# Block 1 of the second token group by seven products, and another order of VectorE's steps in that group

## The chip, the cores and the metric

One of the cores of a Trainium2 chip runs the whole program. The metric is the device time in microseconds (us) of one execution; lower is better.

## The reference

Two blocks follow each other. The first is a chunked state-space layer over 4 batches, 8 heads, 768 positions, head size 32 and state size 16; the second is a feed-forward layer with the quick GELU over all 3072 tokens.

```python
# per chunk: y = (C B^T * L) x + (C state) * exp(cum);  state = decay * state + sum_j B_j x_j decay_j
x = attn_out.transpose(0, 2, 1, 3).reshape(3072, 256)
h = x @ w_in                                  # 256 -> 2048
g = h * (1.0 / (1.0 + np.exp(-1.702 * h)))
out = g @ w_out                               # 2048 -> 256
```

## The kernel before

The 3072 tokens are worked on in six groups of 512 (g = 0 to 5). Each group's rows of the state-space layer are made on TensorE (gain, score and the y steps) while the feed-forward layer of the group before is still running, so that TensorE always has full 128x128 matmuls beside the small 32-row ones. A "pair" is 256 tokens; a group has two pairs.

The feed-forward layer's first product (yT times w_in) has 16 blocks of 128 rows of the hidden layer, taken two by two as j = 0 to 7. It is computed in one of two ways.

- Directly: `hidden` (L887) makes one row block with two matmuls of 512 columns, and ScalarE applies the silu from PSUM to SBUF.
- By seven products instead of eight, on 256 columns each (Strassen's scheme in Winograd's form): `first(g, j, i)` (L931) issues one step named by its letter. Steps 1, 6, 7 and 4 accumulate in bank X, and after 1, 6 and 7 ScalarE copies the running sum out of X (into `ac` or `b`) before the next product may add to it; 4 ends with a silu from X. Steps 5, 2 and 3 accumulate in bank Y. D adds Y and `ac` on VectorE, 3 is followed by an addition of Y and `b` on VectorE, S and T are silus on ScalarE. The sums of weights that the products need come from `mix_in(n)` (L905; n covers blocks 2n and 2n + 1), and the sums of yT from `mix_y(g)` (L924).

The second product (with w_out) is done by seven products as well: `product` (L1028), shown as P in the step lists, with sums from `mix_w(n)` and `mix_g(g, j)`, accumulated in seven half banks called `acc`.

A fp32 matmul is executed as two passes; the profile counts passes.

The state-space steps of a group, by their names in the code: `decay` (a scan on VectorE and two products with b, L424 and L489), `gain` (TensorE, into two banks A), `keep_both` (ScalarE copies out of the A banks, then VectorE additions), `score` (TensorE, into the area cb), `weigh` (VectorE multiplies the decay matrix L by cb, L693), `finish(pairs, (0,))` (TensorE, states into the area y, L822), `finish(pairs, (1,))` (TensorE, weighted rows into y, L836, and then three copies of y into yT on ScalarE, L871 and L869). The areas cb, y and acc are one and the same four banks of PSUM, one after the other. `clip_rows` and `decay_rows` prepare the decay of later rows on VectorE and GpSimd, and `turn_out` (L1111) transposes a half group of results on VectorE and issues four output DMAs on SyncE's queue.

Every engine works in the order of the program: `in_order` (L21) pins each instruction behind the one before it on its engine. The order between steps is written out by hand, in strings of step names that `run` (L1290) goes through. Two places are of importance here. The dictionary `after` (L1263) holds the steps behind the direct blocks of group 1 (H0 behind block 0, H1 behind block 1). The strings of `run(1, ...)` from L1332 on hold the rest of the second group (g = 1); `steady(j)` (L1307) gives the steps for blocks 5 to 7, mixed with the second product's P.

Of the kernel before, what the change touches and what calls it, by code (L numbers as in the profile page):

```python
# [16 lines left out]
P = 128  # L17
# [18 lines left out]
def kernel(  # L36
# [383 lines left out]
    def decay(p):  # L420

        L = ssd.tile([P, 2 * NH * H], FP32, tag="L", name=f"L{p}", bufs=3)
        Ls[p] = L.rearrange("p (k r q i) -> p k r q i", k=2, r=R, q=Q)
        nc.vector.tensor_tensor_scan(  # L424
            out=L, data0=ra[p].rearrange("p k e -> p (k e)"),
            data1=idents.rearrange("p h i -> p (h i)"), initial=0.0, op0=ALU.mult, op1=ALU.add)
        for k in range(2):
            ends(p, k)
# [203 lines left out]
    def turn_blocks(g):  # L632

        t = {}
        for name in "CB":
            t[name] = ssd.tile([P, TG], FP32, tag=f"{name}t", name=f"{name}t{g}", bufs=1)
            nc.vector.transpose(
                out=t[name].rearrange("p (n i f) -> p n f i", n=PG, i=32),
                in_=blocks.pop((name, g)).rearrange("p h (f n) -> p f h n", n=N))
        for n in range(PG):  # L640
            s = st[g * PG + n] = {}
            s["BT"], s["tp"] = (
                t[name][:, n * 2 * P:(n + 1) * 2 * P].rearrange("p (k i) -> p k i", k=2)
                for name in "BC")
# [16 lines left out]
    def since_start(p, engine=nc.vector):  # L661

        b, c = divmod(2 * p, NC)
        s = st[p]
        tp = s["tp"]
        s["CsT"] = ssd.tile([P, 2, P], FP32, tag="CsT", name=f"CsT{p}", bufs=3)
        engine.tensor_tensor(out=s["CsT"], in0=tp, in1=since[b][:, c:c + 2], op=ALU.mult)

    def score(pairs, between=lambda: None, to=None):

        cb = (to or area(f"cb{pairs[0]}")).rearrange("p r (k e) -> p r k e", k=2 * PG)
        for n, p in enumerate(pairs):
            s = st[p]
            BT, CT = s["BT"], s.pop("CT")
            s["cb"] = cb[:, :, 2 * n:2 * n + 2]
            if n:
                between()
            for k in range(2):
                for i, side in enumerate(SIDES):
                    for r in range(R):  # L680
                        rows = slice(32 * r, 32 * r + 32)
                        nc.tensor.matmul(  # L682
                            out=s["cb"][side, r, k].rearrange("p (q i) -> p q i", q=Q),
                            lhsT=BT[rows, k, side], rhs=CT[rows, k, :, side],
                            start=True, stop=True, tile_position=(32 * r, H * i),
                            skip_group_check=True)

    def weigh(p, ks=(slice(0, 2),)):

        Lv = Ls[p].rearrange("p k r q i -> p k r (q i)")  # L690
        cb = st[p]["cb"].rearrange("p r k e -> p k r e")
        for k in ks:
            nc.vector.tensor_tensor(out=Lv[:, k], in0=Lv[:, k], in1=cb[:, k], op=ALU.mult)  # L693
# [7 lines left out]
    def gain(pairs, to=None):  # L701

        A = [(bank(f"A{pairs[0]}_{i}") if to is None else to[:, i, TG // 2:])[
            :, :2 * len(pairs) * Q * D].rearrange("p (k e) -> p k e", e=Q * D) for i in range(2)]
        for n, p in enumerate(pairs):
            Be = BE.pop(p)[0]
            for k in range(2):
                for r in range(R):
                    heads = slice(Q * r, Q * r + Q)
                    for i, side in enumerate(SIDES):  # L710
                        if last_chunk(p, 2 * k + i):
                            continue
                        nc.tensor.matmul(  # L713
                            out=A[i][32 * r:32 * r + 32, 2 * n + k],
                            lhsT=Be[side, k, r],
                            rhs=rx[p][side, k, heads].rearrange("p h d -> p (h d)"),
                            start=True, stop=True, tile_position=(H * i, 32 * r),
                            skip_group_check=True)
            increment[p] = [t[:, 2 * n:2 * n + 2] for t in A] if pairs[0] else A
# [27 lines left out]
    def keep_both(pairs, by_scalar=False):  # L747

        for p in pairs:
            part_of(p, range(4), by_scalar)  # L750
        for p in pairs:
            add_up(p, range(4))
# [148 lines left out]


    mixed_in, mixed_y, chain = {}, {}, {}

    def mix_in(n):  # L905

        t = wide.tile([P, PN], FP32, tag=("m", "p2")[n % 2], name=f"mi{n}").rearrange(
            "p (j s e) -> p j s e", j=2, s=4)
        w = w_in[:, 4 * n:4 * (n + 1)].rearrange("p (j i) k e -> p j i k e", i=2)
        a11, a12, a21, a22 = w[:, :, 0, 0], w[:, :, 0, 1], w[:, :, 1, 0], w[:, :, 1, 1]  # L910
        s1, s2, s3, s4 = (t[:, :, i] for i in range(4))
        for o, u, v, op in ((s1, a21, a22, ALU.add), (s2, s1, a11, ALU.subtract),
                            (s3, a11, a21, ALU.subtract), (s4, a12, s2, ALU.subtract)):
            nc.vector.tensor_tensor(out=o, in0=u, in1=v, op=op)
        for k in range(2):
            mixed_in[2 * n + k] = t[:, k]

    def mix(t, B):

# [4 lines left out]
    def mix_y(g):  # L924
        mixed_y[g] = ffn.tile([P, 4, HT], FP32, tag="my", name=f"my{g}", bufs=1)
        mix(mixed_y[g], yT[g].rearrange("p k (t e) -> p k t e", t=2))
# [184 lines left out]
    def turn_out(g, i):  # L1111

        t = out_tile(g, i).rearrange("p k e -> p (k e)")
        nc.vector.transpose(out=t, in_=sums[g][:, i].rearrange("p t e -> p (t e)"))
        rows = out[g * TG:(g + 1) * TG].rearrange("(b j) d -> j b d", j=32)
        for r in range(R):
            cols = slice(i * P + 32 * r, i * P + 32 * r + 32)
            src = t[32 * r:32 * r + 32].rearrange("p (b e) -> p b e", e=32)
            n = 2 if (g, i) == (NG - 2, 1) and r else 1
            for k in range(n):  # L1120
                bs = slice(16 // n * k, 16 // n * (k + 1))
                nc.sync.dma_start(out=rows[:, bs, cols], in_=src[:, bs])
# [106 lines left out]
    def at(places, i, *work):  # L1229
        places.setdefault(i, []).extend(work)  # L1230
# [9 lines left out]
    for i, k, c in ((2, 1, 1), (3, 2, 3), (4, 4, 7), (5, 8, 10), (6, 10, 14), (7, 14, 15)):  # L1240
# [13 lines left out]
    at(in_project[0], 10, lambda: score(pairs), lambda: gain(pairs), lambda: keep_both(pairs, True),  # L1254
       lambda: weigh(PG), lambda: weigh(PG + 1))
    at(in_project[0], 15, lambda: finish(pairs))
    at(in_project[0], 13, lambda: mix_in(1), lambda: turn_blocks(2), lambda: decay(n))
    at(in_project[0], 6, lambda: spread(n), lambda: spread(n + 1), lambda: load_blocks(n),
       lambda: load_blocks(n + 1), lambda: load(n, "b"), lambda: load(n + 1, "b"),
       lambda: load(n, "x"), lambda: load(n + 1, "x"))  # L1260
# [2 lines left out]
    after = {}  # L1263

    later = n, n + 1
    at(after, "H0", lambda: decay(n + 1), lambda: mix_y(1), lambda: since_start(n),
       lambda: since_start(n + 1), lambda: gain(later), lambda: keep_both(later, True), lambda: score(later),
       lambda: weigh(n), lambda: weigh(n + 1))
    at(after, "H1", lambda: turn_out(0, 0), lambda: turn_out(0, 1), lambda: mix_in(2),
       lambda: mix_w(0))  # L1270
    assert [b for b in range(NB) if 3 * CG <= b * NC < 4 * CG] == [2]


# [7 lines left out]
    load_blocks(p)  # L1281
    spread_rows(2)
    load(p, "bx")
    for step in "H0", "H1":
        for i in range(2):
            hidden(1, 2 * int(step[1:]) + i)
        for do in after[step]:
            do()

    def run(g, steps, products=(), **do):  # L1290


        products = iter(products)
        for step in steps.split():
            if step == "P":
                product(*next(products))
            elif step in do:
                do[step]()
            else:
                j, i = step.split(".")  # L1300
                first(g, int(j), i)
        assert next(products, None) is None
# [24 lines left out]
    def more_loads():  # L1327
# [1 line left out]
        load(p + 1)  # L1329
        spread(p + 1)  # L1330

    run(1, "2.1 3.1 2.5 2.6 3.6 z 2.2 2.7 3.5 3.7 3.2 2.D 2.4 3.D 3.4 2.S W 3.S y m 2.3 3.3 4.1 2.T 3.T",  # L1332
        m=lambda: mix_g(1, 0),
        z=lambda: finish(later, (0,)), y=lambda: finish(later, (1,)), W=lambda: clip_rows(2))
    mix_g(1, 1)
    more_loads()
    mix_in(3)
    decay_rows(2)
    run(1, "4.5 4.2 P P 4.6 P P 4.7 P P P 4.D", seven(1, 0))
    mix_w(1)  # L1340
    mix_g(1, 2)
    decay(p)
    between = {5: (lambda: mix_g(1, 3), lambda: mix_w(2)),
               6: (lambda: mix_g(1, 4), lambda: decay(p + 1)),
               7: (lambda: mix_g(1, 5), lambda: mix_w(3))}
    for j in range(5, NF // 2):
        run(1, steady(j), seven(1, j - 4), M=lambda: [do() for do in between[j]])
    k = NF // 2 - 1
    run(1, closing(k), seven(1, 4))
    mix_g(1, 6)  # L1350
    mix_in(0)
    run(1, "P P A P P P P P", seven(1, 5), A=lambda: ahead(2, p))
    mix_g(1, 7)

# [105 lines left out]
```

## Time and profile before

| what | value |
|---|---|
| median of three runs | 345.67 us (345.42 to 346.44) |
| the profiled execution, its own time | 345.17 us |
| its span, first to last instruction | 343.4 us |
| TensorE busy | 338.3 us, 98% |
| VectorE busy | 255.5 us, 74% |
| ScalarE busy | 155.8 us, 45% |
| granted TensorE clock, mean | 1.00 |

The span and the execution's own time differ by 1.8 us of start and end. The profile's times are counted from the start of the span. In this execution the first group's projection ends at about 78 us, the second group fills the stretch from there to about 124 us, and groups 2 to 5 follow.

### The profile page before, as it was taken

How to read it: one execution, taken by the hardware profiler on the slowest of the kernel's cores; microseconds unless marked ns; L12 is line 12 of the kernel's file. 1: busy time of each engine (PE TensorE's matmuls, PEld its weight loads, DVE VectorE, ACT ScalarE, POOL GpSimd, SP SyncE). 2: the span in 40 equal slices, each digit the busy share in tenths (PEclk: the TensorE clock that was granted, in tenths of full speed). 3: DMA queues.
4: the chain of work that ended last, by engine and by line, in shares of the span. 5: the costliest groups of instructions: out<-in, count | busy, mean ns of one | idle time of the engine just before them, and what ended most of it. 6: DMA issues, size and time to landing. Idle time of an engine off the chain costs nothing.

```text
span 343.4 us, 8128 instructions
## 1 busy us (share of the span) xinstructions
PE 338.3 (98%) x3378; PEld 271.2 (79%) x3378; DVE 255.5 (74%) x486; ACT 155.8 (45%) x356; POOL 13.3 (4%) x40
## 2 busy tenths in 40 slices
PE   8999999999999999999999999999999999999996
PEld 6645744555788888888888888888888888899996
DVE  6989999999999797858995667787564653465463
ACT  5798672406563314554333554342553422554320
POOL 6100010200010000000000000000000000000000
DMA  6699978455737000345513036400000300000402
GB/s 166 138 296 210 323 158 151 107 84 106 116 80 123 7 2 22 56 111 92 108 32 46 2 86 115 63 3 0 2 3 2 61 2 0 0 2 0 63 0 62
DMA packets 90020, 25.75 MB, mean 75 GB/s; under 512 B 73440, under 2 KB 87264, under 8 KB 89984
## 3 DMA queue, kind: packets, MB, share of 16 engines
q1 hardware_dynamic: 89152, 24.72, 34.8%
q8 instruction: 26, 0.43, 0.6%
q10 hardware_dynamic: 832, 0.52, 0.5%
q14 instruction: 10, 0.08, 0.1%
HBM read 21.99 MB, written 3.24 MB: 73 GB/s over the span
## 4 chain that ended last, share of the span: by engine, by line
PE 97%; DMA 1%; ACT 0%; DVE 0%; issue 0%; ACTq 0%; DVEq 0%
PE acc L1057 28%; PE X L952 19%; PE Y L962 15%; PE h L896 10%; PE o L994 8%; PE acc L1064 7%; PE y L836 3%; PE cb L682 2%; PE y L822 1%; PE A L713 1%; PE ab L556 1%; DMA az<-in_a_dram 1%; PE tp L599 0%; DVE cum L359 0%; ACT yT L856 0%
## 5 line engine op out<-in xcount | busy, mean ns | idle before, releaser
L957 ACT ACTIVATE ac<-X 128x256 f32<-128x256 f32 x76 | 29.0, 382 | 83.9 <-PE X L952 83.8
L1057 PE MATMUL acc<-mg,mw 128*128 128x256 f32 x192 | 53.9, 379 | 0.0
L1084 DVE TENSOR_TENSOR gT<-Y,ac 128x512 f32<-128x512 f32 x38 | 26.2, 689 | 37.0 <-PE Y L962 34.5
L929 ACT ACTIVATE gT<-gT 128x512 f32<-128x512 f32 (+1 forms) x76 | 38.9, 519 | 26.1 <-DVE gT L1084 25.5
L952 PE MATMUL X<-my,mi 128*128 128x256 f32 x152 | 45.1, 379 | 0.0
L1057 PEld LDWEIGHTS acc<-mg,mw 128*128 128x128 f32 x192 | 36.5, 190 | 4.9
L1084 DVE TENSOR_TENSOR gT<-Y,b 128x256 f32<-128x256 f32 x38 | 16.0, 420 | 28.7 <-PE Y L962 28.7
L896 PE MATMUL h<-yT,w_in 128*128 128x512 f32 (+1 forms) x96 | 35.1, 524 | 0.5 <-ACT yT L856 0.5
L1057 PE MATMUL acc<-gT,w_out 128*128 128x256 f32 x128 | 35.5, 379 | 0.0
L952 PEld LDWEIGHTS X<-my,mi 128*128 128x128 f32 x152 | 28.2, 190 | 3.6
L896 PEld LDWEIGHTS h<-yT,w_in 128*128 128x128 f32 x96 | 18.1, 190 | 16.0 <-issue 12.4
L994 PE MATMUL o<-gT,w_out 128*128 128x512 f32 x64 | 28.3, 596 | 0.0
L920 DVE TENSOR_TENSOR mg<-gT 128x512 f32<-128x512 f32 x40 | 27.3, 681 | 0.0
L1057 PEld LDWEIGHTS acc<-gT,w_out 128*128 128x128 f32 x128 | 24.4, 190 | 3.3
L957 ACT ACTIVATE b<-X 128x256 f32<-128x256 f32 x38 | 14.6, 383 | 19.2 <-PE X L952 18.5
L962 PE MATMUL Y<-my,mi 128*128 128x256 f32 x76 | 23.0, 384 | 0.0
L952 PE MATMUL X<-my,w_in 128*128 128x256 f32 x76 | 22.8, 384 | 0.0
L962 PE MATMUL Y<-yT,w_in 128*128 128x256 f32 x76 | 22.7, 381 | 0.0
L962 PE MATMUL Y<-yT,mi 128*128 128x256 f32 x76 | 22.6, 381 | 0.0
L994 PEld LDWEIGHTS o<-gT,w_out 128*128 128x128 f32 x64 | 11.9, 190 | 13.6 <-issue 13.1
L952 PE MATMUL X<-yT,w_in 128*128 128x256 f32 x76 | 22.5, 379 | 0.0
L424 DVE TENSOR_TENSOR_SCAN L<-a,idents 128x1024 f32<-128x1024 f32 x9 | 20.5, 2279 | 0.0
(152 smaller groups left out, 546.2 us busy)
## 6 DMA issues: line engine op xcount, KB each, us to landing
a<-scratch SPq DMA_DIRECT2D x18, 256.0 KB, 4.6
bits<-in_moe_w_out_dram SPq DMA_DIRECT2D x8, 512.0 KB, 8.4
x<-in_x_dram SPq DMA_DIRECT2D x24, 128.0 KB, 3.7
out_dram<-ob SPq DMA_DIRECT2D x37, 64.0 KB, 2.0
bits<-in_moe_w_in_dram SPq DMA_DIRECT2D x8, 256.0 KB, 4.8
bits<-in_moe_w_in_dram SPq DMA_DIRECT2D x4, 512.0 KB, 8.9
b<-in_B_dram SPq DMA_DIRECT2D x20, 64.0 KB, 3.5
af<-in_a_dram SPq DMA_DIRECT2D x3, 384.0 KB
```

Source lines behind the costliest of these rows:

```text
L424: nc.vector.tensor_tensor_scan(out=L, data0=ra[p].rearrange("p k e -> p (k e)"), data1=idents.rearrange("p h i -> p (h i)"), initial=0.0, ...
L836: nc.tensor.matmul(out=y[i][t][D * q:D * q + D, 2 * n + k], lhsT=rx[p][side, k, h], rhs=L[side, k, h // Q, h % Q], start=begin(i, t, (q,)) ...
L896: nc.tensor.matmul(out=h[:, cols], lhsT=w_in[:, f, k], rhs=yT[g][:, k, cols], start=(k == 0 and c == 0), stop=(k == NK - 1), skip_group_ch ...
L920: nc.vector.tensor_tensor(out=t[:, 0:2], in0=B[:, :, 1], in1=B[:, 0], op=ALU.subtract)
L929: nc.scalar.activation(o, i, AF.Silu, scale=GELU_SCALE)
L952: nc.tensor.matmul(out=s["X"], lhsT=lhsT, rhs=rhs, start=i == "1", stop=i == "4", skip_group_check=True)
L957: nc.scalar.activation(copy, s["X"], AF.Copy)
L962: nc.tensor.matmul(out=o, lhsT=lhsT, rhs=rhs, start=s.pop("new", False), stop=i != "5", skip_group_check=True)
L994: nc.tensor.matmul(out=o[c], lhsT=w_out[:, c, f], rhs=gT[g, f // 2][:, f % 2], start=(f == 0), stop=(f == NF - 1), skip_group_check=True)
L1057: nc.tensor.matmul(out=acc[g][0][i][:, cols], lhsT=w, rhs=h[:, cols], start=(j == 0 and k == 0 and (i, 0) in begins), stop=(j == NF // 2 - ...
L1064: nc.tensor.matmul(out=o[k] if type(o) is list else o[:, cols], lhsT=h[:, cols], rhs=w, start=(j == 0 and (i, k) in begins), stop=(j == NF ...
L1084: nc.vector.tensor_tensor(out=o, in0=v, in1=w, op=ALU.add)
```

## The change

In the second group (g = 1), block 1 is no longer made by `hidden` but by `first`, as blocks 2 to 7 are. For that, the half of `mix_in(0)` that block 1 needs is made earlier, during the first group's projection, and the other half stays where all of it was. The step list of the group is written anew: blocks 1 and 2 run side by side, and then 3 and 4; the two `weigh` steps leave the list `after` and stand further back among the steps; `mix_in(2)`, `mix_w(0)`, `mix_in(3)`, `mix_g(1, 0)`, `mix_g(1, 1)`, the rows (`clip_rows(2)`, `decay_rows(2)`) and both output turns of group 0 get other places in VectorE's order. `more_loads` now stands ahead of `mix_g(1, 0)`.

```diff
-    def mix_in(n):
+    def mix_in(n, js=slice(0, 2)):
...
-    at(in_project[0], 13, lambda: mix_in(1), lambda: turn_blocks(2), lambda: decay(n))
+    at(in_project[0], 13, lambda: mix_in(1), lambda: mix_in(0, slice(1, 2)),
+       lambda: turn_blocks(2), lambda: decay(n))
...
-    at(after, "H0", lambda: decay(n + 1), lambda: mix_y(1), lambda: since_start(n),
-       lambda: since_start(n + 1), lambda: gain(later), lambda: keep_both(later, True), lambda: score(later),
-       lambda: weigh(n), lambda: weigh(n + 1))
-    at(after, "H1", lambda: turn_out(0, 0), lambda: turn_out(0, 1), lambda: mix_in(2),
-       lambda: mix_w(0))
+    at(after, "H0", lambda: decay(n + 1), lambda: mix_y(1), lambda: first(1, 1, "1"),
+       lambda: first(1, 2, "1"), lambda: since_start(n), lambda: since_start(n + 1), lambda: gain(later),
+       lambda: keep_both(later, True), lambda: score(later))
...
-    for step in "H0", "H1":
-        for i in range(2):
-            hidden(1, 2 * int(step[1:]) + i)
-        for do in after[step]:
-            do()
+    for i in range(2):
+        hidden(1, i)
+    for do in after["H0"]:
+        do()
...
-    run(1, "2.1 3.1 2.5 2.6 3.6 z 2.2 2.7 3.5 3.7 3.2 2.D 2.4 3.D 3.4 2.S W 3.S y m 2.3 3.3 4.1 2.T 3.T",
-        m=lambda: mix_g(1, 0),
-        z=lambda: finish(later, (0,)), y=lambda: finish(later, (1,)), W=lambda: clip_rows(2))
-    mix_g(1, 1)
+    run(1, "1.5 1.6 2.6 1.2 1.7 2.5 2.7 2.2 w 1.D z 1.4 2.D 2.4 1.S 2.S v 1.3 2.3 1.T 2.T m 3.1 3.5 3.6 3.2 4.1 "
+        "M y 3.7 4.5 4.2 3.D 3.4",
+        w=lambda: weigh(n), v=lambda: weigh(n + 1), m=lambda: mix_in(2), M=lambda: mix_w(0),
+        z=lambda: finish(later, (0,)), y=lambda: finish(later, (1,)))
     more_loads()
-    mix_in(3)
-    decay_rows(2)
-    run(1, "4.5 4.2 P P 4.6 P P 4.7 P P P 4.D", seven(1, 0))
-    mix_w(1)
-    mix_g(1, 2)
+    mix_g(1, 0)
+    run(1, "P P 4.6 3.S P 3.3 P G 4.7 P P 3.T P 4.D", seven(1, 0), G=lambda: mix_g(1, 1))
+    mix_w(1)
+    clip_rows(2)
+    mix_g(1, 2)
+    turn_out(0, 0)
+    turn_out(0, 1)
+    mix_in(3)
     decay(p)
...
-        run(1, steady(j), seven(1, j - 4), M=lambda: [do() for do in between[j]])
+        run(1, steady(j, "o" if j == 6 else ""), seven(1, j - 4), M=lambda: [do() for do in between[j]],
+            o=lambda: decay_rows(2))
...
-    mix_in(0)
+    mix_in(0, slice(0, 1))
```

In the program as built, step z stands behind both `weigh` steps on VectorE, since the area y takes the place of cb; on VectorE itself the second `weigh` stands behind the additions 1.D and 2.D.

## The prediction

> **What bounds the kernel now.** I read the page's busy shares and its chain first, then a table of stretches, then each engine's rows around the second group (78 to 124 us).
>
> ```profile
> PE 338.3 (98%) x3378; PEld 271.2 (79%) x3378; DVE 255.5 (74%) x486; ACT 155.8 (45%) x356; POOL 13.3 (4%) x40
> ...
> PE 97%; DMA 1%; ACT 0%; DVE 0%; issue 0%; ACTq 0%; DVEq 0%
> ```
>
> The chain is TensorE almost alone. The stretches (stretch, length, then busy us of PE, PEld, DVE, ACT and POOL with their counts) show that TensorE never idles between 17.6 and 330 us, and how full VectorE is where the change lies:
>
> ```profile
> 17.60:78.20 60.60, 60.60 (x457) 31.94 (x458) 57.47 (x90) 34.05 (x58) 3.97 (x6) 1.00 0.80 188
> 78.20:124.00 45.80, 45.80 (x487) 36.37 (x485) 41.86 (x84) 22.11 (x56) 1.40 (x3) 1.00 0.44 78
> 124.00:330.00 206.00, 206.00 (x1881) 181.15 (x1881) 136.18 (x269) 86.46 (x216) 0.32 (x2) 1.00 0.20 36
> ```
>
> So a matmul saved in the second group shortens the end by its own length, and a wait put before a matmul lengthens it by its own length. VectorE is busy for 41.86 of 45.80 us there: its order decides who waits.
>
> Rows that carry the sum (start us, us, engine, line, tiles, count), first TensorE's, then ScalarE's, then VectorE's:
>
> ```profile
> 83.65 3.70 PE L896 MATMUL h<-yT,w_in 128*128 128x512 f32 x8
> 87.19 1.03 PE L952 MATMUL X<-yT,w_in 128*128 128x256 f32 x4
> 88.05 0.60 PE L962 MATMUL Y<-my,mi 128*128 128x256 f32 x2
> 93.50 1.48 PE L836 MATMUL y<-L,x 64*32 64x64 f32 x128
> ```
> ```profile
> 95.02 0.60 ACT L871 ACTIVATE yT<-y 128x512 f32<-128x512 f32 x1
> 95.63 1.19 ACT L869 ACTIVATE yT<-y 64x512 f32<-64x512 f32 x2
> 96.84 0.38 ACT L957 ACTIVATE ac<-X 128x256 f32<-128x256 f32 x1
> ```
> ```profile
> 85.54 2.35 DVE L693 TENSOR_TENSOR L<-L,cb 128x1024 f32<-128x1024 f32 x2
> 87.80 1.30 DVE L1114 STREAM_TRANSPOSE ob<-c 128x512 f32<-128x512 f32 x2
> ...
> 101.08 0.67 DVE L1084 TENSOR_TENSOR gT<-Y,ac 128x512 f32<-128x512 f32 x1
> 101.66 0.42 DVE L1017 TENSOR_TENSOR mw<-w_out 128x256 f32<-128x256 f32 x1
> 103.13 0.69 DVE L920 TENSOR_TENSOR mg<-gT 128x512 f32<-128x512 f32 x1
> 104.65 2.28 DVE L424 TENSOR_TENSOR_SCAN L<-a,idents 128x1024 f32<-128x1024 f32 x1
> 107.38 0.42 DVE L1084 TENSOR_TENSOR gT<-Y,b 128x256 f32<-128x256 f32 x1
> ```
>
> The reader is to see the pitches. A product (two passes of 256 columns) takes 0.43 us of TensorE and its result is complete 0.60 after its start. Back to back, VectorE steps cost the distance to the next start: D 0.60, mix_w 1.47 (101.66 to 103.13), mix_g 1.52, decay 2.73 (104.65 to 107.38), two output turns 1.22 (87.80 to 89.02). From an earlier wait, the h matmul at 17.58 released by ScalarE at 17.52, I take 0.05 us for a release and 0.10 for a longer first pass.
>
> **The matmuls.** Block 1 loses eight 512-wide passes: 83.65 to 87.19 is 3.54, less 0.09 for leaving 32-row tiles, 3.45 us. It gains seven products, 7 x 0.432 = 3.02. That is 0.43 us off the path. ScalarE and VectorE get copies, additions (0.69 and 0.42) and silus for it; their cost appears only as waits, below.
>
> **Covered moves, at nothing.** The half of mix_in(0) in the first group's projection puts four 128-column additions before VectorE's second-group preparations: between 0.21 each (the pitch of the 128-column products at 107) and 0.28, about 0.9 us. Cover: the last decay factors, ready at 80.7, become 81.6; gain reaches them at 82.9. The y sums move from 82.3 to 83.2; product 5 wants them at 84.6. The output turns' eight DMA issues go behind the loads on SP; the scan that needs those loads comes some 10 us after the memset that frees their buffer (a mix_g, 1.52, and 8.6 us listed under wait 5), and an "a" load lands in 4.6 us. GpSimd's part of clip_rows (1.4 us busy in the whole stretch) has over 8 us before decay_rows. If that cover failed, each costs its excess, under 1 us.
>
> **Wait 1, product 1.5.** Its bank is one of gain's, which ScalarE must read out first. Gain starts two products later (81.71 + 0.86 = 82.57); with its 0.80 and score's 1.14 that is 84.51, and 1.5 could go at 84.6. ScalarE's eight copies (1.69 us from 82.64 now) start at 83.50; the sixth is the last from that bank and ends at 84.80; with release 84.95. Cost 0.4, between 0.1 and 0.7.
>
> **Wait 2, step z.** The area y takes over the scores' banks, so z waits until both weigh steps have read them. The second weigh now stands behind 1.D and 2.D on VectorE. From the start t of product 2.2: result t+0.60, 2.D t+0.65, weigh t+1.26, its end t+2.47, z t+2.62. TensorE is there at t+0.52. Cost 2.1, between 1.9 and 2.3: it hangs on no absolute time. Before, both weighs ended at 87.9 and z came at 89.4.
>
> **Wait 3, product 3.6.** It waits for ScalarE's copy of 3.1, which is queued behind two X silus, 1.S, 2.S, 1.T and 2.T. In the trace such a series, counted from the start of 1.4's counterpart at 92.54, has its two 512-wide silus from 93.89 to 95.03; two 256-wide ones (0.31 pitch) and the copy then end at 95.93, 3.39 later; 3.6 starts at +3.54. TensorE gets there after six products, +2.59. Cost 0.95, between 0.6 and 1.1.
>
> **Wait 4, product 3.4.** The copy of 3.7 is issued behind step y, so it queues behind the three yT activations. Counted from y's first matmul at 93.50, the copy after those three ends at 97.22, +3.72, and 3.4 starts at +3.87; TensorE, with y (1.41), a switch and three products, is there at +2.80. Cost 1.1, between 0.8 and 1.3. Before, the first copy behind them was 4.1's, and 4.6 came seven products after y.
>
> **Wait 5, product 6.6.** It waits for the copy of 6.1, which ScalarE holds behind 4.T, which waits for VectorE's addition 4.3. VectorE's queue from 3.3's addition (at t+0.65, t the start of product 3.3): 0.34, mix_g(1,1) 1.52, 4.D 0.61, mix_w(1) 1.47, clip 0.47, mix_g(1,2) 1.52, turns 1.22, mix_in(3) 1.43, decay 2.73, then 4.3's addition 0.42: t+12.38. 4.T's pitch 0.30, the copy 0.38, release: 6.6 at t+13.24. TensorE is 24 products further at t+10.37. Cost 2.9, between 2.2 and 3.5 (5% on 12.4 us of pitches either way). The same queue now goes from 4.D at 101.08 to 107.38, and the copy ended at 108.52 for a matmul at 108.83. The three steps put in (clip, turns, mix_in) are worth 3.1 us against that slack of 0.3.
>
> **A rule weighed.** The trace shows a slow clock once: eight equal 128x256 bf16 passes at L550 start 0.213 us apart, then 0.109, the change coming 3.4 us after the first matmul. The longest new wait, 2.9 us, comes near that length.
> The Trainium skill, "TensorE: Matmul & The Clock Gate", section "What's actually happening", says that TensorE's clock halves after an idle window of about 3.4 us; by it the five waits leave the clock alone.
>
> **Sum.** 0.4 + 2.1 + 0.95 + 1.1 + 2.9 - 0.43 = 7.0 us. Made against the profiled execution (span 343.40, time 345.17) that is 352.2; the median of the runs, 345.67, is 0.5 above that one, so I predict 352.7 (with every wait at its lower or upper bound +5.2 to +8.5, that is 350.9 to 354.2).
>
> **Rivals.** *Given back:* the waits are real, but the lead that VectorE gains is used up later, so that only the 0.43 us stays: 345.2. Its place is TensorE's idle time after 124 us; it decides from 6 us of it on. The table shows 206.00 busy of 206.00. Chance 0.06 (0.01 of it beyond 0.3%). *No fifth wait:* VectorE runs further ahead than I count, so that 4.3's addition comes in time: 352.7 - 2.9 = 349.8. Against it: 3.3's addition waits for its product, which ties VectorE to TensorE just there. Chance 0.05. *Halved clock:* the fifth wait grows past 3.4 us (0.5 more), and for one such stretch products take 0.86 instead of 0.43, 1.7 us more: 354.9. Chance 0.06. *The change doesn't do what it says:* the built order has the seven products of block 1 and none of its 512-wide ones, so this gets no chance of its own.
>
> **How the numbers follow.** The forecast has 0.83. The range 349.8 to 354.6 holds it with its bounds and the case without the fifth wait; outside lie the given-back case, the halved clock and tails. About 0.3%, 1 us, is what a measurement of this kernel tells from no change: faster 0.01, same 0.05, slower 0.94.
>
> **What would show it.** Right: TensorE idle 7 to 8 us between 82 and 116 us, in five pieces, the largest before 6.6 (released by ScalarE, behind a VectorE addition to gT) and before z (released by VectorE's weigh); still none after 124. Wrong: z within 0.5 us of 2.2, the 6.1 copy not behind 4.T, or products over 0.43 us apart after a wait.

## The result and the profile after

The changed kernel takes 353.73 us (median of five runs, 353.42 to 354.47), the kernel before 345.42 us beside it (344.83 to 346.44): a ratio of 1.024, 95% interval 1.0218 to 1.0262. It is 8.3 us slower. The prediction was 352.7 us, with 349.8 to 354.6 as its range.

The profiled execution took 353.51 us, with a span of 351.8. From the page after, the busy shares, the chain, and the granted clock in 40 slices of 8.8 us:

```profile
PE 341.1 (97%) x3384; PEld 273.4 (78%) x3384; DVE 257.2 (73%) x492; ACT 157.3 (45%) x360; POOL 13.4 (4%) x40
...
PE 93%; DVE 4%; ACT 2%; issue 0%; DVEq 0%
...
PEclk9999999999899999999999999999999999999999
```

The six passes that TensorE has more than before (eight of 512 columns gone, fourteen of 256 come) are there, and so are the steps of VectorE that now take 4% of the chain. New is the 8 in the clock: one slice, from 88 to 97 us, had less than the full clock. The table of stretches (the column before the last two is the granted clock) says the same, and that all the lost time lies in the second group:

```profile
78.20:124.00 45.80, 39.76 (x455) 31.36 (x454) 36.31 (x75) 20.89 (x56) 1.41 (x3) 0.96 0.44 78
124.00:340.00 216.00, 216.00 (x1935) 189.71 (x1934) 145.10 (x286) 89.55 (x223) 0.33 (x2) 1.00 0.19 35
```

Before, TensorE was busy for all 45.80 us of that stretch. Now it idles for 6.0 us of it, and after 124 us for none, as before. What TensorE waited for (us in total, times, longest):

```profile
PE X L955 <- ACT ac L960: 3.7, 3, 2.6
PE y L822 <- DVE L L693: 2.1, 1, 2.1
...
PE Y L965 <- ACT S L767: 0.3, 1, 0.3
```

None of these three stood in the list of before. They are the five waits of the prediction (these lines are three higher than before: X is L955, Y L965, the copy L960, the addition L1087). TensorE's rows show each in its place, with its releaser in brackets:

```profile
84.99 0.70 PE L965 MATMUL Y<-my,mi 128*128 128x256 f32 x2 [0.31 <-ACT S L767]
...
88.12 0.59 PE L965 MATMUL Y<-yT,w_in 128*128 128x256 f32 x2
90.78 0.90 PE L822 MATMUL y<-CsT,S 32*64 32x64 f32 x64 [2.07 <-DVE L L693]
91.62 1.85 PE L955 MATMUL X<-my,w_in 128*128 128x256 f32 x4
93.26 1.91 PE L965 MATMUL Y<-yT,mi 128*128 128x256 f32 x4
...
96.41 0.70 PE L955 MATMUL X<-my,mi 128*128 128x256 f32 x2 [0.25 <-ACT ac L960]
...
101.69 0.70 PE L955 MATMUL X<-my,w_in 128*128 128x256 f32 x2 [0.81 <-ACT ac L960]
...
113.88 0.59 PE L1060 MATMUL acc<-gT,w_out 128*128 128x256 f32 x2
117.07 0.70 PE L955 MATMUL X<-my,mi 128*128 128x256 f32 x2 [2.60 <-ACT ac L960]
```

The rows at 91.62 and 93.26 are the surprise: four passes take 1.85 and 1.91 us where the same four took 1.03 before. No wait is shown there; TensorE runs at half its clock (0.50 from 91.9 to 95.3 us, in the table under "Where the clock halves").

VectorE's rows for the wait before z (2.D's addition, then the second weigh) and for the one before 6.6 (turns, scan of the decay, 4.3's addition), and ScalarE's two behind that addition (4.T, then 6.1's copy):

```profile
88.82 0.69 DVE L1087 TENSOR_TENSOR gT<-Y,ac 128x512 f32<-128x512 f32 x1 [0.26 <-PE Y L965]
89.43 1.21 DVE L693 TENSOR_TENSOR L<-L,cb 128x1024 f32<-128x1024 f32 x1
...
110.49 1.30 DVE L1117 STREAM_TRANSPOSE ob<-c 128x512 f32<-128x512 f32 x2
...
113.14 2.29 DVE L424 TENSOR_TENSOR_SCAN L<-a,idents 128x1024 f32<-128x1024 f32 x1
...
115.88 0.42 DVE L1087 TENSOR_TENSOR gT<-Y,b 128x256 f32<-128x256 f32 x1
```
```profile
116.33 0.42 ACT L932 ACTIVATE gT<-gT 128x256 f32<-128x256 f32 x1 [5.32 <-DVE gT L1087]
116.65 0.37 ACT L960 ACTIVATE ac<-X 128x256 f32<-128x256 f32 x1
```

ScalarE stood idle for 5.32 us before 4.T, and 6.1's product (the X product at 112.58 us) had been complete since 113.2 us: VectorE's queue is what TensorE waited for.

**Where the 8.2 us went.** I take the distance from one TensorE start to the next, less the distance when nothing waits, and add 0.10 for a longer first pass after a wait. For 6.6 that is 117.07 - 113.88 - 0.43 + 0.11 = 2.87.

| term | predicted | measured |
|---|---|---|
| 1, product 1.5 | 0.4 | 0.38 |
| 2, step z | 2.1 | 2.14 |
| half clock, 91.9 to 95.3 us | 0 | 1.68 |
| 3, product 3.6 | 0.95 | 0.51 |
| 4, product 3.4 | 1.1 | 1.08 |
| 5, product 6.6 | 2.9 | 2.87 |
| block 1 | -0.43 | -0.42 |
| sum | 7.0 | 8.24 |

The next gain of TensorE starts 8.35 us later than before (132.38 against 124.03), 0.13 of which was there at 78 us already: 8.22.

The five waits sum to 6.98 us here, and the idle time in the list of waits to only 6.04: the profile counts a product as busy for 0.60 us, up to 0.17 beyond the time at which the next one could start, and the longer first pass is no idle time.

### The profile page after: what moved, and what is told of

It is laid out like the page before. It is cut to its first block, busy times and chain, and to the rows that moved or that the text cites. A ratio compares the mean times of both kernels' runs of the same rounds, so it can differ in the third digit from the quotient of the medians.

```text
span 351.8 us, 8150 instructions
## 1 busy us (share of the span) xinstructions
PE 341.1 (97%) x3384; PEld 273.4 (78%) x3384; DVE 257.2 (73%) x492; ACT 157.3 (45%) x360; POOL 13.4 (4%) x40
## 4 chain that ended last, share of the span: by engine, by line
PE 93%; DVE 4%; ACT 2%; issue 0%; DVEq 0%
PE acc L1060 26%; PE X L955 19%; PE Y L965 14%; PE h L896 9%; PE o L997 8%; PE acc L1067 7%; PE y L836 3%; PE cb L682 2%; PE y L822 1%; PE A L713 1%; PE ab L556 1%; PE busy L468 1%; DVE gT L1087 1%; DVE L L424 1%; PE ab L550 0%
## 5 line engine op out<-in xcount | busy, mean ns | idle before, releaser
L960 ACT ACTIVATE ac<-X 128x256 f32<-128x256 f32 x78 | 29.8, 382 | 82.4 <-PE X L955 82.3
L1087 DVE TENSOR_TENSOR gT<-Y,ac 128x512 f32<-128x512 f32 x39 | 26.9, 689 | 39.1 <-PE Y L965 33.4
L932 ACT ACTIVATE gT<-gT 128x512 f32<-128x512 f32 (+1 forms) x78 | 40.0, 519 | 30.2 <-DVE gT L1087 29.7
L955 PE MATMUL X<-my,mi 128*128 128x256 f32 x156 | 46.6, 381 | 2.8 <-ACT ac L960 2.8
L1087 DVE TENSOR_TENSOR gT<-Y,b 128x256 f32<-128x256 f32 x39 | 16.4, 420 | 33.3 <-PE Y L965 33.3
L955 PEld LDWEIGHTS X<-my,mi 128*128 128x128 f32 x156 | 28.7, 190 | 7.3 <-ACT ac L960 3.6
L896 PE MATMUL h<-yT,w_in 128*128 128x512 f32 (+1 forms) x88 | 31.5, 517 | 0.5 <-ACT yT L856 0.5
L896 PEld LDWEIGHTS h<-yT,w_in 128*128 128x128 f32 x88 | 16.5, 190 | 14.6 <-issue 11.2
L955 PE MATMUL X<-my,w_in 128*128 128x256 f32 x78 | 24.3, 397 | 0.8 <-ACT ac L960 0.8
L965 PE MATMUL Y<-my,mi 128*128 128x256 f32 x78 | 23.7, 385 | 0.3 <-ACT S L767 0.3
L965 PE MATMUL Y<-yT,mi 128*128 128x256 f32 x78 | 23.9, 392 | 0.0
L960 ACT ACTIVATE b<-X 128x256 f32<-128x256 f32 x39 | 15.0, 384 | 19.9 <-PE X L955 19.4
L955 PE MATMUL X<-yT,w_in 128*128 128x256 f32 x78 | 23.2, 381 | 0.0
L965 PE MATMUL Y<-yT,w_in 128*128 128x256 f32 x78 | 23.2, 379 | 0.0
```

The source lines that it names most:

```text
L896: nc.tensor.matmul(out=h[:, cols], lhsT=w_in[:, f, k], rhs=yT[g][:, k, cols], start=(k == 0 and c == 0), stop=(k == NK - 1), skip_group_ch ...
L932: nc.scalar.activation(o, i, AF.Silu, scale=GELU_SCALE)
L955: nc.tensor.matmul(out=s["X"], lhsT=lhsT, rhs=rhs, start=i == "1", stop=i == "4", skip_group_check=True)
L960: nc.scalar.activation(copy, s["X"], AF.Copy)
L965: nc.tensor.matmul(out=o, lhsT=lhsT, rhs=rhs, start=s.pop("new", False), stop=i != "5", skip_group_check=True)
L1087: nc.vector.tensor_tensor(out=o, in0=v, in1=w, op=ALU.add)
```

## The experiments

The first four ran on one chip beside runs of the kernel before (345.66 us), the next three on another (345.78), the last two on a third (346.23, a single execution). Sizes of waits are worked out as above, without the 0.10. Because the half clock comes in some executions and not in others, each execution's mean granted clock is told where it matters: 0.995 means one such stretch of 3.41 us.

**Both weighs ahead of 1.D** (`e1_both_weighs`), for the wait before z alone:

```diff
-    ... "w 1.D z 1.4 2.D 2.4 1.S 2.S v 1.3 ..."   w=lambda: weigh(n), v=lambda: weigh(n + 1)
+    ... "w 1.D z 1.4 2.D 2.4 1.S 2.S 1.3 ..."     w=lambda: (weigh(n), weigh(n + 1))
```

> The changed kernel with the second weigh put back directly behind the first, ahead of 1.D and 2.D. Theory (five waits made by the order, and a halved clock made by the idle time before z): the two weighs end 86.5 + 1.13 + 1.21 = 88.85, z starts near 89.0 where TensorE is at 88.64, so the wait before z falls from 2.14 to about 0.4; too little idle time to halve the clock, so 1.68 comes back, of which the wait before 3.6 takes 0.44 again. Time 353.73 - 1.8 - 1.7 + 0.4 = 350.7. Rival A (the clock falls for another reason than this idle time): 351.9. Rival B (the seven products of block 1 and their extra work on VectorE and ScalarE are the cost, not the order): 353.7, no change.

Measured: 351.84 us (ratio 1.0194, 1.0154 to 1.0233). The list of what TensorE waited for now has, for z:

```profile
PE y L822 <- DVE L L693: 0.3, 1, 0.3
```

In the profiled execution the clock stayed at 1.0, wait 3 was 0.83 (0.93 with the longer pass, as predicted), wait 5 unchanged at 2.76, and the time 351.02. The other three had a clock of 0.995 and took 351.67 to 353.5. So the second weigh's place is the cause of wait 2. The profiled time lies beside the theory's 350.7. The median lies on rival A's 351.9, and rival A is right in this: three of the four executions have a slow stretch without the long wait before z. The theory had no other cause for it.

**Four steps out of VectorE's queue** (`e2_queue_of_decay`), for wait 5 alone: `clip_rows(2)`, both turns and `mix_in(3)` stand behind `mix_w(0)`.

```diff
-        w=lambda: weigh(n), v=lambda: weigh(n + 1), m=lambda: mix_in(2), M=lambda: mix_w(0),
+        ..., M=lambda: [do() for do in (lambda: mix_w(0), lambda: clip_rows(2), lambda: turn_out(0, 0),
+                                 lambda: turn_out(0, 1), lambda: mix_in(3))],
...
     mix_w(1)
-    clip_rows(2)
     mix_g(1, 2)
-    turn_out(0, 0)
-    turn_out(0, 1)
-    mix_in(3)
     decay(p)
```

> The changed kernel with clip_rows(2), both output turns and mix_in(3) moved from the queue in front of decay to the place behind mix_w(0), where VectorE idles 3.1 us before 3.D. Theory: the three are 0.47 + 1.22 + 1.43 = 3.1 us and fit into that idle time; the wait before 6.6 (2.87) goes, the other four waits and the halved clock stay: 353.73 - 2.9 = 350.9. Rival (VectorE is simply overloaded in this group, and the wait comes back at a later step): 353 or more, with a new wait of TensorE for VectorE after 102 us.

Measured: 349.87 us (ratio 1.0126, 1.0091 to 1.016). Wait 5 fell from 2.76 to 0.64, not to nothing. VectorE's rows of the profiled execution show what is late next:

```profile
111.03 2.29 DVE L424 TENSOR_TENSOR_SCAN L<-a,idents 128x1024 f32<-128x1024 f32 x1 [0.92 <-DMA a<-scratch]
...
113.77 0.42 DVE L1087 TENSOR_TENSOR gT<-Y,b 128x256 f32<-128x256 f32 x1
```

VectorE, now early enough, idles 0.92 us before the scan for a transfer of the scan's rows. That transfer is late by this experiment's own move: the turns also issue the eight output DMAs, which now stand ahead of the loads on SyncE's queue (SPq). First its rows here, then the changed kernel's issue of the same loads:

```profile
99.69 4.99 SPq L1125 DMA_DIRECT2D out_dram<-ob  x8
104.77 1.27 SPq L275 DMA_DIRECT2D a<-scratch  x2
```
```profile
102.41 1.26 SPq L275 DMA_DIRECT2D a<-scratch  x2
```

The loads are issued 2.36 us later. Without the 0.92 the product 6.6 could have started at 114.04, before TensorE was there (114.32). So by these rows VectorE's order makes all of wait 5, and the 0.64 that is left belongs to the new place of the turns; no run moves the two other steps without the turns. Four of the six executions ran at the full clock (349.31 to 350.04), two at 0.995 (351.41 and 351.64). The theory's 350.9 had one slow stretch and no wait; the profiled execution, with one slow stretch, lies 0.5 above it, and the median lies below it because most executions had no slow stretch.

**TensorE kept busy before z** (`e3_zero_products`): five products with weights of zero, added to 1's running sum, stand before z, so that nothing that is computed changes.

```diff
+    nil = const.tile([P, P], FP32, name="nil")
+    nc.gpsimd.memset(nil, 0.0)
...
+        for _ in range(5):
+            nc.tensor.matmul(out=chain[1, 1]["X"], lhsT=nil, rhs=mixed_y[1][:, 3], start=False, stop=False, ...)
...
-    ... "w 1.D z 1.4 ..."
+    ... "w 1.D Z z 1.4 ..."
```

> The changed kernel with five more products before z: their weights are all zero and they add to block 1's X, so that nothing changes but TensorE's occupation (5 x 0.43 = 2.16 us, as long as the wait). Theory (the idle time before z halves the clock): z starts as before near 90.8, the clock stays at 1.00, the products after z are 0.43 apart; 1.68 comes back and the wait before 3.6 grows by 0.44: 353.73 - 1.2 = 352.5. Rival A (the clock falls for another reason, the 32-row matmuls of z for example): products 0.85 apart all the same, 353.7. Rival B (z does not wait for the second weigh but only comes late on TensorE): the five products come on top, 355.9.

Measured: 356.08 us (ratio 1.0297, 1.0254 to 1.0339). The profiled execution took 353.8. TensorE's rows of it, the zero products and z:

```profile
88.07 2.32 PE L1339 MATMUL X<-my,nil 128*128 128x256 f32 x10
90.32 0.91 PE L822 MATMUL y<-CsT,S 32*64 32x64 f32 x64
```

TensorE did not idle before z, the clock stayed at 1.0, and wait 3 was back at 0.83. z started 2.68 us after product 2.2 (2.66 in the changed kernel), so the five products fill the wait and do not come on top of it: rival B is refuted by the trace, although the median lies beside its 355.9. It lost 1.84 us at 260.9 us to a step y that waited for nothing that the profile shows; without it this execution comes to 352.0, near the theory's 352.5. That no slow stretch follows z when its wait is filled fits the theory that the idle time halves the clock, but the next experiment shows that this execution alone proves little. The three unprofiled executions had a clock of 0.995 and took 356.1 to 356.4. One slow stretch is worth 1.7; where the rest of their 4 us over 352 went, no trace shows, so the median of this run is not accounted for.

**3.7 ahead of step y** (`e4_copy_before_y`), so that its copy is not queued behind the three yT activations:

```diff
-        "M y 3.7 4.5 4.2 3.D 3.4"
+        "M 3.7 y 4.5 4.2 3.D 3.4"
```

> The changed kernel with product 3.7 put ahead of step y, so that its copy is ahead of the three yT activations on ScalarE. Theory: 3.4 no longer waits, but acc takes over the banks of y, and the first P waits for the same three activations: y starts 0.43 later, yT is done 3.3 us after y's start, TensorE is at the first P 2.8 us after it, so a wait of 0.5 to 0.8 stands at P instead of 1.08 at 3.4: 353.73 - 0.4 = 353.3, a difference that the runs can hardly tell; the trace tells it. Rival (the wait just goes): 352.6.

Measured: 352.26 us (ratio 1.0202, 1.0162 to 1.0242). The wait at 3.4 is gone. In its place the first P waits for the last yT activation:

```profile
PE acc L1060 <- ACT yT L869: 0.4, 1, 0.4
```

That is 0.57 lost instead of 0.97: 0.4 of wait 4 is won, the rest turns into a wait for y's banks, as the theory had it. The times don't tell this from the rival, whose 352.6 is as near; the trace does. Two executions ran at the full clock (351.88, 351.14), two at 0.995 (353.64, 352.64). The profiled one was at the full clock although it idles 2.1 us before z; that opened the question of the clock, below.

**VectorE's order alone, in the kernel before** (`e6_queue_alone`): block 1 stays with its eight passes, and only three steps are moved.

```diff
-    at(after, "H1", lambda: turn_out(0, 0), lambda: turn_out(0, 1), lambda: mix_in(2),
-       lambda: mix_w(0))
+    at(after, "H1", lambda: mix_in(2), lambda: mix_w(0))
...
-    mix_in(3)
...
     mix_g(1, 2)
+    turn_out(0, 0)
+    turn_out(0, 1)
+    mix_in(3)
     decay(p)
```

> The kernel before, with block 1 of the first product still by eight 512-wide passes; only VectorE's order is changed: the two output turns of group 0 and mix_in(3) stand between mix_g(1,2) and decay(p), where the changed kernel has them, so that 2.65 us more of VectorE's work is ahead of the addition 4.3. Theory (the fifth wait is made by VectorE's order, not by the seven products): before has 0.3 us of slack there, so TensorE waits 2.1 to 2.6 us before product 6.6, released by ScalarE's copy behind 4.T; no other new wait; the time is that of the kernel before plus 2.1 to 2.6 (about 348.0), and 1.7 more in an execution in which the clock halves after the wait. Rival (the wait comes from the added copies, additions and silus of the seven products): without them VectorE has the room, the wait is under 0.5 us and the time within 0.5 us of the kernel before.

Measured: 347.74 us (ratio 1.0053, 1.0029 to 1.0076), 1.96 over the kernel before. The wait is there, before 6.6, without the seven products:

```profile
PE X L952 <- ACT ac L957: 1.6, 1, 1.6
```

It costs 1.72, less than the 2.1 to 2.6 expected. Taken from their old place, the steps let VectorE start 4.D's addition at 100.71 instead of 101.08 us (after 0.68 of idle time for a copy by ScalarE), and TensorE itself came to 6.6 0.32 later than before (109.15 against 108.83); 2.65 less these two and less the slack of 0.3 is 1.65. All five executions ran at the full clock.

**The seven products without the waits** (`k3_seven_without_waits`): block 1 as in the changed kernel, the lists written anew. Among the rest, `decay(p)` now stands behind 4.3's addition (d, in the list of block 6):

```diff
-    at(after, "H0", lambda: decay(n + 1), lambda: mix_y(1), lambda: first(1, 1, "1"),
-       lambda: first(1, 2, "1"), lambda: since_start(n), ...
+    at(after, "H0", lambda: decay(n + 1), lambda: mix_y(1), lambda: since_start(n), ...
...
+    run(1, "1.1 2.1 1.5 1.6 2.6 1.2 1.7 2.5 2.7 w 1.D 1.4 2.2 2.D 2.4 3.1 z 1.S 2.S 1.3 2.3 m 3.5 1.T 2.T 3.6 3.2 4.1 "
+        "M t 3.7 3.D u C y q 4.5 4.2 3.4 4.6 3.3 L",
+        w=lambda: (weigh(n), weigh(n + 1)), ..., C=lambda: clip_rows(2),
+        t=lambda: turn_out(0, 0), u=lambda: turn_out(0, 1), i=lambda: mix_in(3), q=lambda: mix_g(1, 0), ...)
+    run(1, "P P 3.S P P G 4.7 P P 3.T P i 4.D", seven(1, 0), G=lambda: mix_g(1, 1), i=lambda: mix_in(3), ...)
...
-    decay(p)
...
+        run(1, steady(j, {6: "d", 7: "o"}.get(j, "")), ..., o=lambda: decay_rows(2), d=lambda: decay(p))
```

> Block 1 of group 1 by seven products, as in the changed kernel, with the order of the steps made so that no wait of TensorE is left behind: 1.1 and 2.1 as products after the scores, both weighs ahead of 1.D, step z seven products after them, clip, the output turns and the mixed weights ahead of mix_g(1,0), 3.4's copy ahead of step y, mix_in(3) behind the last first product of block 3, decay(p) behind 4.3's addition. Theory (the seven products save their 0.42 us, and all that the change lost is waits, 7.0 us, with the clock that they halve, 1.7): TensorE has no idle stretch over 0.3 us after 78 us, the clock stays at 1.0, and the time is 0.2 to 0.4 us under that of the kernel before. Rival (the additions, copies and silus of the seven products are more than VectorE and ScalarE have room for in this group): some wait of 0.5 us or more appears between 82 and 124 us whatever the order, and the time is that of before or longer.

Measured: 345.27 us against 345.78 (12 and 18 executions; ratio 0.9989, 0.9969 to 1.0009), clock 0.999 or 1.0 in all. From TensorE's first start after 78 us to the next group's gain, the stretch of this kernel and then that of the kernel before:

```profile
78.22:123.63 45.41, 45.41 (x493) 37.51 (x491) 42.12 (x87) 23.03 (x59) 1.40 (x3) 1.00 0.44 78
```
```profile
78.18:124.03 45.85, 45.85 (x488) 36.38 (x486) 41.91 (x84) 22.11 (x56) 1.40 (x3) 1.00 0.44 78
```

TensorE is busy throughout in both, and the group is 0.44 us shorter. ScalarE's and VectorE's additional work fits in. The saving is real in the trace; the times alone can't tell it from none. This is the only version with block 1 by seven products that isn't slower than the kernel before.

**Where the clock halves** (`a7_after_again`, the changed kernel; `e8_fifth_wait_clock` and `e9_fifth_wait_clock`, the kernel with both weighs ahead of 1.D, on a third chip):

> The changed kernel itself, one more profiled execution, to see where the clock halves. Theory (the granted clock follows the idle share of fixed stretches of 3.41 us whose beginnings differ from one execution to the next, and halves for the next stretch when about 2.0 us or more of one are idle): either the wait before z (2.1 us) or that before 6.6 (2.9 us) falls mostly into one stretch, and the 3.41 us at half clock begin within 3.4 us after it; if after 6.6, wait 3 is back to 0.8 to 0.95 us; the time is about 353.5. Rival (z alone halves the clock, by what TensorE does there, not by how the idle time falls): the slow stretch begins again between 90.8 and 94.2 us.

> The kernel with both weighs ahead of 1.D once more (no long wait before z, the 2.6 us of idle before product 6.6 still there), for one more profiled execution, to see where the clock halves in it. Theory (the granted clock is set anew every 3.413 us, counted from the moment it first became full; it halves for the next 3.413 us when more than about 2.0 us of such a stretch were idle): the wait before 6.6 lies with more than 2.0 us in one stretch in some 6 of 10 executions; then the slow stretch begins within 1 us of the wait's end, a whole number of 3.413 us after the first full clock, and TensorE loses 1.7 us to it; otherwise the clock stays full. Rival (only the wait before z can halve it): no slow stretch at all.

> The same kernel once more, for another place of the 3.413 us stretches: the same expectations. Theory: a slow stretch behind the wait before 6.6 if and only if more than about 2.0 us of that wait's idle time lie in one stretch. Rival: no slow stretch.

Measured: a7 354.52 us profiled (355.01 median of two, ratio 1.0266, 1.0232 to 1.03), e8 352.26, e9 351.12. In a7 the slow stretch again followed z, at 92.26 us, which fits its theory and its rival alike. In e8, which hardly idles before z (0.28), it followed the wait before 6.6, so z is not needed for it. In e9 no product is slow (after the same 2.76 before 6.6 they start 0.43 apart).

In the trace's record of the granted clock, it first became full at 6.56 us in the changed kernel, 6.92 in a7, 5.82 in e2 and 4.75 in e8. The slow stretch began 85.33, 85.34, 85.33 and 109.22 us after that: 25, 25, 25 and 32 times 3.413. Each lasted 3.41. So in these four executions the clock is set anew at fixed steps of 3.413 us, whose phase differs between executions. Here are the stretch that ended with the halving and the slow one, in the changed kernel, then in e8 (stretch, length, PE busy first; clock before the last two columns):

```profile
88.48:91.89 3.41, 1.34 (x67) 1.07 (x66) 1.90 (x3) 0.22 (x1) 0.00 (x0) 1.00 0.45 72
91.89:95.30 3.41, 3.41 (x9) 2.72 (x9) 0.52 (x2) 2.12 (x5) 0.00 (x0) 0.50 0.02 5
```
```profile
110.56:113.97 3.41, 0.82 (x5) 0.39 (x3) 3.38 (x6) 0.78 (x3) 0.00 (x0) 1.00 0.93 176
113.97:117.39 3.42, 3.42 (x8) 2.80 (x9) 3.17 (x9) 1.10 (x3) 0.00 (x0) 0.50 0.44 69
```

And the stretch of e4 that holds most of its idle time before z, after which the clock stayed full (24 steps after the first full clock at 5.36 us):

```profile
87.27:90.69 3.42, 1.48 (x7) 0.95 (x5) 2.99 (x4) 0.77 (x2) 0.00 (x0) 1.00 0.76 106
```

Idle for 2.07 us of 3.41 (the changed kernel, a7 and e2 alike) or for 2.59 (e8): half clock next. Idle for 1.94 (e4): none. In the changed kernel the 2.60 us before 6.6 fell across a step, 1.31 and 1.29, and did nothing. The ends of the kernels, where TensorE runs out of work, agree, with the steps counted in the same way: the step after 2.29 us (the changed kernel), 2.46 (e6), 2.52 (e1) or 2.73 (e4) of idle time has half the clock, the step after 1.65 (a7) or 1.71 (e8) the full one. So the limit lies between 1.94 and 2.07 us. In each of these steps nearly all the idle time was one gap; whether several short gaps add up, no run shows. A wait split by a step would also account for e9, but its record has no change of the clock from which to count the steps, so for e9 it is not shown.

## Why the prediction was right, and where it was not

**Slower, and by waits of TensorE in the second group: right.** Five waits of the predicted places and releasers, none after 124 us. That they, with the slow stretch that they bring, are the whole loss is shown by k3: the same products without the waits take no longer than before. The releasers of waits 2, 4 and 5 were each moved by a run of their own; for waits 1 and 3 the rows and k3 have to do. Two of the prediction's own signs did not hold: TensorE idled 6.0 us in the five pieces, not 7 to 8, and after the wait before z products stood 0.85 apart, which it had named as a sign of being wrong.

**The sizes: four of five within 0.05 us.** Each followed the series of its step. For z, from the start of 2.2 at 88.12: 2.D at +0.70, weigh at +1.31, z at +2.66, where the prediction had 0.65, 1.26 and 2.62. For 6.6, from 3.3's product at 103.95: TensorE was ready at +10.36 and started at +13.12, where it had 10.37 and 13.24. Counting from the product that ties VectorE to TensorE, instead of from absolute times, is why the errors of earlier terms did not add up.

**Block 1, -0.43: right**, -0.42 here and -0.44 in k3. The covered moves cost nothing that shows.

**The clock: the step that failed.** The prediction weighed each wait's length against 3.4 us, found 2.9 below it, and gave the halved clock 0.06, at the fifth wait only. Its 3.4 us came from a row where the clock rose after the first work; no row of before showed how much idle time lowers it. The trace has it after the second one, 2.07 us of idle, for 1.68 us. The rule drawn on, the Trainium skill, "TensorE: Matmul & The Clock Gate", section "What's actually happening", states a window of 3413 ns that runs freely, and an idle window as the condition. The length and the free running agree with this trace (3.41 us, 25 steps after the first full clock); that the whole window has to be idle does not, since 1.34 us of work in it did not keep the clock. Read as a limit on one gap or on a whole window, the rule leaves the clock alone at 2.07 us; the measurement decides against it.

**Wait 3, 0.95: mis-sized by the same step.** At the full clock it is 0.93 (e1, e3 and e4 with the longer pass). Here TensorE came to it late from the slow stretch, so only 0.51 was left; ScalarE, too, waited there, 0.47 for a slow product and 0.44 for the addition behind one, where it runs without a gap in e1 and e4. The clock's cost in the end is 1.68 - 0.42 = 1.26, which is the difference of the sums (8.24 against 7.0) and, with a kernel before that ran 0.25 us faster beside this one (345.42 against 345.67), the 1.0 us by which the median missed.

**The rivals.** *Given back* is refuted: no idle time after 124 us takes up any of it. *No fifth wait* is refuted by 2.87 us, and e2 and e6 show that VectorE's order makes that wait. *Halved clock* came true in its price (1.7) but at another wait and by another condition. It had been put at 354.9, outside the range. That 353.73 lies inside although the clock halved is luck: wait 3 took back 0.42, the fifth wait did not grow by the 0.5 that this rival needed, and the kernel before ran 0.25 faster.

**By chance or not?** All seven executions of the changed kernel had a mean clock of 0.990 to 0.995, so each had at least one slow stretch; the two that were profiled had it after z. Two waits that are long enough, 26 us apart, give the steps two chances. As an estimate, with the limit at 2.0 us: z's 2.07 puts that much into one step for 1.48 of the 3.41 us of possible places (0.43), the 2.60 before 6.6 for 2.01 (0.59). A kernel with z's wait alone and 0.5 of idle time before 6.6 (e2) had a slow stretch in two of six executions, those with the wait before 6.6 alone (e1, e3, e8 and e9) in seven of ten. So a chance of 0.06 was far too low. One of 18 executions of the kernel before had a clock of 0.995 too (348.02 us); it was not profiled, and its cause stays open.

## What to carry to other kernels

Where one engine is the bound, write for each new wait the series that releases it, counted from the last event that ties the releasing engine to the bound one; a step put into another engine's queue costs its time less the slack there, and less what the steps before it gain from its absence (2.65 us of steps cost 1.72 in e6). The order of the steps can be the whole loss while the arithmetic saved is still a gain (k3): repair the order before judging the idea. Ask of a new wait how much idle time it can put into one stretch of 3.4 us of TensorE: 2.07 us in one such stretch cost another 1.7, and whether it falls into one stretch differs between executions.

## What the runs showed of the hardware that was not expected

TensorE's clock halved for 3.41 us after a stretch of 3.413 us with 2.07 us of idle in it (busy 39%), and not after one with 1.94 (busy 43%). Whether the same wait does it hangs on where the steps fall in that execution, which spreads the times of one kernel: e2 took 349.31 to 350.04 us at the full clock and 351.41 to 351.64 with one slow stretch.

Step y, 128 small matmuls, lost over 1 us in two traces to nothing that TensorE waits for in the profile (1.84 us at 260.9 us in e3, 1.24 at 149.7 in e6). In both, a transfer on the queues that the profile calls "instruction" lay beside the loss (260.41 to 261.34 us in e3, 149.78 to 150.09 in e6), but one did so too where nothing was lost (262.10 to 263.39 in the changed kernel, whose step y at 261.39 took the usual 1.41). Its cause stays open.
